# Windowed attention into a gated MLP: a second queue for the block means, another load order, and an order chosen among 64

## The chip, the cores and the metric

The kernel runs on one core of a Trainium2 chip. The metric is the time of the program on the device in microseconds, lower is better. A core has five engines that run side by side, each its own list of instructions in order: TensorE (PE, matrix products), VectorE (DVE), ScalarE (ACT), GpSimd (POOL) and SyncE (SP, which here only issues transfers). Transfers are issued by SP and by ACT; an engine that issues one first waits until the transfer may start, and what stands behind in its list waits too.

## The reference

Four batches of 768 tokens, eight heads of 64. Attention sees two sets of keys: the keys within 16 tokens of the query, and one summary per block of 32 tokens, the maximum of its keys with the mean of its values. An MLP follows, on 3072 tokens of width 512.

```python
k_sum = k.reshape(B, H, nb, block, D).max(axis=3)      # block = 32
v_sum = v.reshape(B, H, nb, block, D).mean(axis=3)
scores_l = where(|i - j| < 16, scale * q @ k.T, -1e9)
scores_s = scale * q @ k_sum.T + log(block)
a = softmax(concat([scores_l, scores_s]))
x = a @ concat([v, v_sum])                             # heads side by side: (3072, 512)
h = x @ w_in                                           # (3072, 1024)
s = h * softmax(h)
ln = (s - mean(s)) / sqrt(var(s) + 1e-6) * g_ln
out = ln @ w_out                                       # (3072, 512)
```

## The kernel before, in words

The work is cut into twelve groups (batch `b`, third `g` of the sequence), each of four query tiles of 64 rows, and each group into two halves `pp` of four heads. A half gives one tile `s` of scores (L555; for the first group straight from `kraw` and `ksum`, else from `kw`, which gathers the windows of keys and the maxima). DVE adds the mask and takes the row minimum (L574), ACT the exponentials (L582), DVE or POOL divides (L265), PE transposes (`t`, L610), ACT or DVE copies to `at`, and PE multiplies with the value tile (`x`, L649). The value tile `vt` of a group holds 96 window rows per query tile, loaded by SP (L512), and below them the 24 block means (`load_v2`, L518), which are copied from `vsum` by a transfer that ACT issues. That transfer writes into the same tile, so it is ordered behind the load.

Each group gives two MLP tile rows of 128 tokens, 24 in all: `h` (L674, two halves of 12 products: four slices of w_in, each in three passes of high and low parts), softmax and centring (L684 to L716; `hm` is the maximum, `he` the tile), transposes `lt` (L610), `lh`/`ll` as high and low part, and `o` (L752, 24 products), which is scaled (L757 or L759) and stored. `o` lags `h` by four tile rows. Both weight matrices come in as words that ACT, DVE and POOL first convert (L345 to L360, L265) and split into a high and a low part (`w`; for w_out L377 and L379). The eight pieces of w_out are thus converted while the first tile rows run, in two buffers that they share with the rows of V that POOL adds for the later batches' means (`st_v`, L478).

Block means are made by PE from rows of V (`vs_ps` with `st_v`, L436) for the first batch, likewise (L449) for the second, and by POOL's sums and PE for the last two.

Nothing runs in the order in which it is written. Every step is recorded with a cost, the engines it could run on, and what it depends on; `Plan.issue` then plays the engines forward. Each engine takes the step that can start first, ties going to the smaller `due` (the earliest place in the program of a PE step that depends on it); `DEAR` is added to an engine's cost where a step could go to several. A transfer is taken to start 1 us after its issue, to move at 410 GB/s (270 at first), and to land 0.6 us later. Where the plan leaves PE idle before 80 us, `keep_up` fills in products with a tile of zeros (L877), so that PE keeps busy; the result is overwritten. `LOADS` sets in which order SP issues the first loads: `k` keys of a pair of heads, `q` queries, `w` a piece of w_in, `r` rows of V for the means, `v` the first value tile, `Q` and `V` the second group's. SP's list is one queue, in order.

Of the kernel before, what the change touches and what calls it, by code (L numbers as in the profile page):

```python
# [2 lines left out]

# [19 lines left out]
NB = S // BLOCK  # L23
# [15 lines left out]
NHE = 5  # L39
EARLY = 3  # L40
MEANS = 2
DIRECT = 0
NEAR = 6
WPT = 2


LOADS = "kqkkqkwwwwwwwwrrrvQV"
NEG = -8.0e9
SCALE = 1.0 / math.sqrt(D)

# [22 lines left out]
class Plan:  # L73
# [4 lines left out]


    RATE, SLOW = 410.0, 270.0  # L80
    START = 0.7
    COLD, FILL = 6.9, 80.0
    IDLE = 0.22
    WAIT, FAR = 1.5, 200
    DEAR = {"dve": 0.6, "act": 0.3, "pool": 1.0}
    SYNC = 0.13

    def __init__(self):
        self.ops, self.rings, self.banks, self.idle = [], {}, {}, None
# [15 lines left out]
    def op(self, engine, cost, fn, r=(), w=(), nbytes=0, after=(), alt=(), port=False):  # L105

        deps = set(after)

        def of(table, part):
            for k, v in table.items():
                if part is None or k is None or k == part:
                    deps.update(v)

        o = Op({e: (c, f) for e, c, f in ((engine, cost, fn), *alt)}, deps,
               len(self.ops), nbytes, port)
        r = [x if isinstance(x, tuple) else (x, None) for x in r]
        w = [x if isinstance(x, tuple) else (x, None) for x in w]
        for b, part in r:  # L120
            of(b.writers, part)
        for b, part in w:
            of(b.writers, part)
            of(b.readers, part)
            for p in b.prev:
                deps.update(p.ops)
                p.gone = True
        assert not any(b.gone for b, _ in r + w)
        for b, part in r:
            b.readers.setdefault(part, []).append(o)  # L130
            b.ops.append(o)
        for b, part in w:
            b.writers.setdefault(part, []).append(o)
            b.ops.append(o)
        deps.discard(o)
        self.ops.append(o)
        return o

    def issue(self):
        ready, free, then, dma, held = {}, {}, {}, 0.0, 0.0  # L140
        for o in self.ops:
            o.left = len(o.deps)
            for d in o.deps:
                d.users.append(o)
        for o in reversed(self.ops):
            o.due = min([u.due for u in o.users] + ([o.prio] if "pe" in o.can else []), default=o.prio)
            if "sp" in o.can:
                o.due = o.prio

        def enter(o):  # L150
            for e in o.can:
                at = max((d.end + (0.0 if d.engine == e == "pe" else self.SYNC) for d in o.deps), default=0.0)
                ready.setdefault(e, []).append((at, o))

        def begin(e, at):
            return max(free.get(e, self.START), at)

        def cost(e, o, t):
            other = free.get("pool", 0.0) if e == "dve" and o.port else held if e == "pool" else 0.0
            return o.can[e][0] * (2 if e == "pe" and t < self.COLD else 1) + max(other - t, 0.0)  # L160

        def loss(e, o, t):
            return cost(e, o, t) + self.DEAR.get(e, 0.0)

        def take(e):

            if e in then:
                return next(((begin(e, at), o) for at, o in ready[e] if o is then[e]), None)
            best = None
            for at, o in ready[e]:  # L170
                t = begin(e, at)
                if any(begin(f, at) + loss(f, o, t) < t + loss(e, o, t) for f in o.can if f != e):
                    continue
                if best is None or t < best[0] - 1e-6 or (t < best[0] + 1e-6 and (o.due, o.prio) < (best[1].due, best[1].prio)):
                    best = (t, o)
            if best is None:
                return None

            t, o = best
            for at, y in ready[e]:  # L180
                s = begin(e, at)
                if t < s and s - t < self.WAIT * (t + cost(e, o, t) - s) and y.due + self.FAR < best[1].due:
                    best = (s, y)
            return best

        for o in self.ops:
            if not o.left:
                enter(o)
        order = []
        while len(order) < len(self.ops):  # L190
            t, e, o = min(((x[0], e, x[1]) for e in ready for x in [take(e)] if x),
                          key=lambda x: (x[0], x[2].due))
            for f in o.can:
                ready[f] = [x for x in ready[f] if x[1] is not o]
            then.pop(e, None)
            if o.then:
                then[e] = o.then
            o.start, o.engine, (o.cost, o.fn) = t, e, o.can[e]
            o.end = free[e] = t + cost(e, o, t)
            if e == "dve" and o.port:  # L200
                held = o.end
            if o.nbytes:
                dma = max(dma, o.end + 1.0)
                dma += o.nbytes / (self.RATE if dma > self.COLD else self.SLOW) * 1e-3
# [6 lines left out]
        at, done = self.START, set()  # L211
        for o in order:
            if o.engine == "pe":
                while at + self.SYNC < min(o.start, self.FILL):
                    at += self.keep_up(at, done)
                at = max(at, o.start) + o.cost * (2 if o.start < self.COLD else 1)
            done.add(o)
            o.fn()

    def keep_up(self, at, done):  # L220

# [10 lines left out]
def attn_then_solu(ctx: ExitStack, tc: tile.TileContext, q, k, v, vr, vb, w_in, w_out, g_ln, out):  # L232
# [281 lines left out]

    def load_v2(b, g):
        x, y = vt[b, g], vsum[b]

        return op(act, 0.8, lambda: nc.scalar.dma_start(  # L518
            out=x.ap[WIN:KC], in_=y.ap[WIN:KC, :].rearrange("p (o c) -> p o c", o=1).broadcast_to([NB, G, DM])),
                  r=[y], w=[(x, 1)], nbytes=NB * 8192)  # L520

    def scores(b, g, pp, direct=False, each=False):

# [290 lines left out]
    step = lambda i: (*its[i // 2], i % 2)  # L814
    for t in range(NT):
        n, j = divmod(t, 2)
        b, g = its[n]
        near = t >= NEAR
        if not near:
            run(scores(*step(t + 2), t < DIRECT))  # L820
# [100 lines left out]
```

## Time and profile before

| | |
|---|---|
| time, median of 3 | 408.04 us (407.03 to 408.69) |
| profiled execution | 406.69 us, span 404.9 us, granted TensorE clock 0.99 |
| PE busy | 388.3 us (96%) |
| of that, products with zeros | 21.6 us in 82 instructions |
| DVE, ACT, POOL busy | 300.5, 230.5, 88.8 us |
| DMA | 49.24 MB, the queue of SP 40.12, that of ACT 8.51 |

The first `h` product starts at 36.31 us, the first `o` product at 74.81. From 136 us on a tile row takes some 14.4 us of PE work, nearly without a wait. A row of the PE timeline names in brackets how long the engine was idle before it and what ended that.

### The profile page before, as it was taken

The numbers are of one execution on the slowest core, as the hardware profiler recorded it, in microseconds if no ns is written. First come the engines' busy times: TensorE is split into PE (matmuls) and PEld (weight loads), VectorE is DVE, ScalarE is ACT, GpSimd is POOL, SyncE is SP. The second block draws the span as 40 slices with busy tenths as digits, with TensorE's granted clock in tenths as the row PEclk, the third lists the DMA queues.
The fourth block names the chain that finished last, engine by engine and source line by source line (L and its number), as shares of the span: only waits on it lengthen the run. The fifth ranks groups of instructions, "written<-read, shape, count | busy, mean of one in ns | idle before, by whom it ended". The sixth has DMA issues, their size and how long they took to land.

```text
span 404.9 us, 9684 instructions
## 1 busy us (share of the span) xinstructions
PE 388.3 (96%) x3702; PEld 299.6 (74%) x3702; DVE 300.5 (74%) x933; ACT 230.5 (57%) x711; POOL 88.8 (22%) x231
## 2 busy tenths in 40 slices
PE   7999999986988999998999999999999999999996
PEld 3436667664876788887888888878878888888776
DVE  4998999989887886776877777687678766654430
ACT  2967788963898664565455664646545453423311
POOL 3020240305581412216202211201201221011100
PEclk9999999996999999999999999999999999999999
DMA  8999992044257040044350040141130000000011
GB/s 270 411 409 364 404 336 75 25 123 152 86 186 258 26 159 28 28 176 126 108 182 21 28 182 2 40 169 42 41 137 2 28 28 26 2 26 28 26 53 52
DMA packets 14994, 49.24 MB, mean 122 GB/s; under 512 B 1836, under 2 KB 2092, under 8 KB 13412
## 3 DMA queue, kind: packets, MB, share of 16 engines
q1 hardware_dynamic: 10112, 40.12, 27.4%
q10 hardware_dynamic: 4836, 8.51, 6.9%
q8 instruction: 29, 0.48, 0.5%
q14 instruction: 17, 0.14, 0.1%
HBM read 40.11 MB, written 6.29 MB: 115 GB/s over the span
## 4 chain that ended last, share of the span: by engine, by line
PE 71%; DMA 12%; DVE 11%; ACT 3%; issue 1%; POOL 1%; SPq 0%; ACTq 0%; POOLq 0%
PE o L752 32%; PE h L674 23%; PE x L649 5%; PE s L555 4%; DMA kraw<-in_k 3%; DMA qt<-in_q 3%; PE lt L610 3%; DMA raw<-in_w_in 2%; PE t L610 2%; DMA vt<-in_v 2%; DMA st_v<-in_vb 1%; DVE e L265 1%; DVE e L574 1%; DVE hm L684 1%; DVE ksum L416 1%
## 5 line engine op out<-in xcount | busy, mean ns | idle before, releaser
L752 PE MATMUL o<-w,lh 128*128 128x512 f32 (+1 forms) x400 | 129.6, 393 | 4.8 <-DVE w L379 4.8
L674 PE MATMUL h<-w,xh 128*128 128x512 f32 x384 | 125.6, 396 | 0.0
L582 ACT ACTIVATE e<-e,nm 128x120 f32<-128x120 f32 x192 | 73.1, 385 | 40.2 <-DVE nm L574 31.1
L752 PEld LDWEIGHTS o<-w,lh 128*128 128x128 f32 x400 | 74.6, 189 | 23.9 <-DVE w L379 5.6
L674 PEld LDWEIGHTS h<-w,xh 128*128 128x128 f32 x384 | 72.1, 188 | 17.4 <-DVE he L697 0.5
L752 PE MATMUL o<-w,ll 128*128 128x512 f32 (+1 forms) x200 | 77.3, 386 | 0.0
L674 PE MATMUL h<-w,xl 128*128 128x512 f32 x192 | 75.5, 393 | 0.0
L684 DVE TENSOR_REDUCE hm<-h 128x1 f32<-128x512 f32 x48 | 32.7, 684 | 33.8 <-PE h L674 33.5
L716 POOL TENSOR_SCALAR ss<-ss 128x1 f32<-128x1 f32 x24 | 6.4, 268 | 167.7 <-ACT sq L712 151.9
L752 PEld LDWEIGHTS o<-w,ll 128*128 128x128 f32 x200 | 38.0, 190 | 6.4
L674 PEld LDWEIGHTS h<-w,xl 128*128 128x128 f32 x192 | 36.1, 188 | 7.8 <-DVE xl L655 0.3
L574 DVE CUSTOM_DVE_ANT_0 e<-s,mask 128x120 f32<-128x120 f32 x192 | 40.6, 276 | 0.1
L689 ACT ACTIVATE he<-h,hm 128x512 f32<-128x512 f32 x48 | 32.8, 691 | 13.9 <-DVE hm L686 13.9
L258 ACT COPY at<-t 120x512 f32<-120x512 f32 x29 | 16.3, 585 | 35.6 <-PE t L610 35.1
L582 ACT ACTIVATION_READ_ACCUMULATOR e<-e,nm 128x1 f32 x192 | 36.4, 190 | 0.0
L697 DVE SCALAR_TENSOR_TENSOR he<-h,hz,he 128x512 f32<-128x512 f32 x48 | 34.2, 744 | 0.2
L737 DVE TENSOR_TENSOR ll<-lt,lh 128x512 fp32r<-128x512 f32 x48 | 31.6, 679 | 0.2
L649 PE MATMUL x<-at,vt 120*64 120x64 f32 (+1 forms) x768 | 28.3, 225 | 0.4 <-DVE at L259 0.4
L265 DVE TENSOR_TENSOR e<-e,z 128x960 f32<-128x960 f32 x24 | 28.5, 1189 | 0.1
L478 POOL TENSOR_TENSOR st_v<-st_v 96x512 f32<-96x512 f32 (+3 forms) x28 | 22.1, 791 | 29.2 <-DMA st_v<-in_vb 28.5
L649 PEld LDWEIGHTS x<-at,vt 120*64 120x64 f32 (+1 forms) x768 | 24.6, 138 | 5.2 <-issue 2.3
L712 ACT ACTIVATE sq<-he 128x1024 bf16<-128x1024 f32 x24 | 25.2, 1050 | 5.3 <-DVE hm L684 2.7
(93 smaller groups left out, 504.2 us busy)
## 6 DMA issues: line engine op xcount, KB each, us to landing
vt<-in_v SPq DMA_DIRECT2D x12, 1024.0 KB, 6.2
kraw<-in_k SPq DMA_DIRECT2D x16, 400.0 KB, 8.5
out<-os ACTq DMA_DIRECT2D x23, 256.0 KB, 2.1
qt<-in_q SPq DMA_DIRECT2D x11, 512.0 KB, 5.4
raw<-in_w_in SPq DMA_DIRECT2D x8, 512.0 KB, 10.1
raw<-in_w_out SPq DMA_DIRECT2D x8, 512.0 KB, 10.1
st_v<-in_vr SPq DMA_DIRECT2D x6, 512.0 KB
st_v<-in_vb SPq DMA_DIRECT2D x8, 384.0 KB, 3.4
```

The source lines that it names most:

```text
L265: by = {dve: lambda: nc.vector.tensor_tensor(out=to(), in0=a(), in1=b(), op=kind), pool: lambda: nc.gpsimd.tensor_tensor(out=to(), in0=a() ...
L478: op(pool, 0.15 + w * 0.0021, lambda w=w, o=o: nc.gpsimd.tensor_tensor(out=o.ap[:n, :w], in0=x.ap[:n, :w], in1=x.ap[:n, w:2 * w], op=ALU.add),
L574: nc.vector.tensor_tensor_reduce(out=e.ap[:, n, :], in0=sc.ap[:, j, (2 * i + up) * KC:(2 * i + up + 1) * KC], in1=mask[:, mi, :], scale=-S ...
L582: nc.scalar.activation(out=e.ap[:, n, :], in_=e.ap[:, n, :], func=AF.Exp, bias=nm.ap[:, n:n + 1], scale=-1.0, accum_out=z.ap[:, n:n + 1])
L649: nc.tensor.matmul(xp()[j * D:(j + 1) * D, i, qs], vs.ap[:k, u, cs], at.ap[:k, u % 2, n[j] + u // 2, :], start=not apart, stop=not apart o ...
L674: nc.tensor.matmul(hp.ap, a.ap[:, c, ts], w.ap[:, i], start=(c == 0 and n == 0), stop=(c == NKC - 1 and n == 2))
L684: op(dve, 0.6, lambda i=i, hp=hp: nc.vector.tensor_reduce(out=nms.ap[:, i:i + 1], in_=hp.ap, op=ALU.max, axis=AX.X, negate=True), r=[hp], ...
L689: op(act, 0.71, lambda i=i, hp=hp: nc.scalar.activation(out=part(i), in_=hp.ap, func=AF.Exp, bias=nm.ap, accum_out=zs.ap[:, i:i + 1]), r=[ ...
L697: op(dve, 0.67, lambda i=i, hp=hp: nc.vector.scalar_tensor_tensor(out=part(i), in0=hp.ap, scalar=zs.ap[:, 0:1], in1=part(i), op0=ALU.mult, ...
L712: op(act, 1.13, lambda: nc.scalar.activation(out=sq.ap, in_=e.ap, func=AF.Square, accum_out=ss.ap), r=[e], w=[sq, ss])
L737: op(dve, 0.6, lambda part=part, r=r: nc.vector.tensor_tensor(out=part(lo), in0=tp.ap[:, r], in1=part(hi).bitcast(F32), op=ALU.subtract), ...
L752: nc.tensor.matmul(o.ap[:, cols], a.ap[:, f, :], w.ap[:, i, cols], start=(f == 0 and n == 0), stop=(f == NFC - 1 and n == 2))
```

## The change

Six things change together.

- `load_v2`: from the second batch on, SP issues the transfer of the block means (at the plan's cost of 0.43 us) and not ACT (0.8 us). The two of the first batch stay with ACT.
- `LOADS`: two pieces of w_in are listed ahead of the first keys, and others are set between the keys and the rows of V.
- `LATE`: the plan lets a transfer that ends after 50 us land 2.0 us after its data and not 0.6.
- `DEAR["dve"]`: 1.0 and not 0.6, so a step that could run elsewhere leaves DVE sooner.
- `issue`: the old loop is now `order`. It runs 64 times, 63 of them with normal noise (3.0, in places of the program) on every `due`, and the order is kept whose last PE step ends first by the plan. An order that gets stuck is dropped.
- `DIRECT` (zero) and its argument go; that changes nothing.

```diff
-LOADS = "kqkkqkwwwwwwwwrrrvQV"
+LOADS = "wwkwqkkkqwwwrrrwwvQV"
+    LATE = 50.0
-    DEAR = {"dve": 0.6, "act": 0.3, "pool": 1.0}
+    DEAR = {"dve": 1.0, "act": 0.3, "pool": 1.0}
+    TRIES, NOISE = 64, 3.0
...
+        due, best = [o.due for o in self.ops], None
+        for seed in range(self.TRIES):
+            noise = random.Random(seed)
+            for o, x in zip(self.ops, due):
+                o.due = x + (noise.gauss(0.0, self.NOISE) if seed else 0.0)
+            order = self.order()
+            if order:
+                end = max(o.end for o in order if "pe" in o.can)
+                if best is None or end < best[0]:
+                    best = end, order, [(o.start, o.end, o.engine, o.cost, o.fn) for o in self.ops]
...
-                o.end = dma + 0.6
+                o.end = dma + (0.6 if dma < self.LATE else 2.0)
...
     def load_v2(b, g):
         x, y = vt[b, g], vsum[b]
-
-        return op(act, 0.8, lambda: nc.scalar.dma_start(
+        e, cost, queue = (sp, 0.43, nc.sync) if b else (act, 0.8, nc.scalar)
+        return op(e, cost, lambda: queue.dma_start(
```

Which engine runs what also changes. Over the program DVE makes 2 `at` copies instead of 19, 18 centrings of `he` instead of 36, and 11 output scalings instead of 18; ACT and POOL have the rest (POOL 11 centrings instead of 1). PE's list has the same products, and 83 products with zeros instead of 82: 72 of them before the first `h` product, where there were 64.

The start of SP's list (`raw` is a piece of a weight matrix as it comes in, `qt` queries, `st_v` rows of V). Before:

```order
L407 DMA kraw_0_93<-in_k 128x800
L506 DMA qt_0_99<-in_q 128x512
L407 DMA kraw_0_93<-in_k 128x800
L407 DMA kraw_1_102<-in_k 128x800
L506 DMA qt_0_99<-in_q 128x512
L407 DMA kraw_1_102<-in_k 128x800
L333 DMA raw_106<-in_w_in 128x1024
```

and with the change:

```order
L356 DMA raw_93<-in_w_in 128x1024
L430 DMA kraw_0_99<-in_k 128x800
L529 DMA qt_0_101<-in_q 128x512 x2
L430 DMA kraw_0_99<-in_k 128x800
L356 DMA raw_105<-in_w_in 128x1024
L356 DMA raw_107<-in_w_in 128x1024
L356 DMA raw_109<-in_w_in 128x1024
L430 DMA kraw_1_111<-in_k 128x800 x2
```

One piece of w_in is first, three more come before the second pair of keys; the rows of V, which were transfers 15 to 17, are 13, 14 and 18.

The end of the conversion of w_out. ACT's list before (`cv_1280` is the last piece, `vt_1_1229` the value tile of the second batch's second group):

```order
L258 CAST lh_1262<-lt_1212 128x8x64
L518 DMA vt_1_1229<-vsum_896 24x4x512
L345 ACTIVATE cv_1280<-raw_272 128x512
L377 ACTIVATE w_1291<-cv_1254,g_sb 128x512
L377 ACTIVATE w_1309<-cv_1280,g_sb 128x512
```

PE's list with the change, where the last piece (`w_1366`) is used for the first time; before, all products of pieces 5 to 8 stood together, with the score group `s_0_1` behind them:

```order
L775 MATMUL o_1118<-w_1258,ll_1072 128x512
L775 MATMUL o_1118<-w_1258,lh_1059 128x512
L633 MATMUL t_0_0_1325<-ident,e_0_0_1132 120x64 x16
L578 MATMUL s_0_1_1344<-kw_0_1_1041,qt_0_536 64x120 x16
L672 MATMUL x_0_0_1376<-at_0_0_1361,vt_0_849 64x64 x16
L775 MATMUL o_1118<-w_1366,lh_1059 128x512
L775 MATMUL o_1118<-w_1366,ll_1072 128x512
```

The transfer of means is gone from this place of ACT's list (on SP it now stands behind one load of rows of V, ahead of the queries of the group after), and transposes, a score group and an `x` stand between the last two pieces.

SP's list around the third value tile, before:

```order
L506 DMA qt_0_624<-in_q 128x1024
L506 DMA qt_2_656<-in_q 128x1024
L512 DMA vt_2_663<-in_v 128x2048
L407 DMA kraw_0_665<-in_k 128x800 x2
L407 DMA kraw_1_696<-in_k 128x800 x2
L407 DMA kraw_0_711<-in_k 128x800 x2
```

and with the change:

```order
L529 DMA qt_0_536<-in_q 128x1024
L430 DMA kraw_0_603<-in_k 128x800 x2
L529 DMA qt_2_698<-in_q 128x1024
L535 DMA vt_2_717<-in_v 128x2048
L430 DMA kraw_0_722<-in_k 128x800 x2
L430 DMA kraw_1_733<-in_k 128x800 x2
```

The first two keys of the third batch (`kraw_0_711`, now `kraw_0_603`) were last of these and are now ahead of the third group's queries and value tile.

More of the change, by code (lines that the diff above doesn't have):

```diff
@@ L1 @@
 import math
+import random
 from contextlib import ExitStack
@@ L41 @@
 MEANS = 2
-DIRECT = 0
 NEAR = 6
 WPT = 2
-LOADS = "kqkkqkwwwwwwwwrrrvQV"
+LOADS = "wwkwqkkkqwwwrrrwwvQV"
 NEG = -8.0e9
@@ L139, in issue @@
     def issue(self):
-        ready, free, then, dma, held = {}, {}, {}, 0.0, 0.0
         for o in self.ops:
-            o.left = len(o.deps)
             for d in o.deps:
@@ L148, in issue, with order @@
                 o.due = o.prio
+        due, best = [o.due for o in self.ops], None
[8 more added lines that the diff above has]
+                    best = end, order, [(o.start, o.end, o.engine, o.cost, o.fn) for o in self.ops]
+        _, order, kept = best
+        for o, x in zip(self.ops, kept):
+            o.start, o.end, o.engine, o.cost, o.fn = x
+        at, done = self.START, set()
+        for o in order:
+            if o.engine == "pe":
+                while at + self.SYNC < min(o.start, self.FILL):
+                    at += self.keep_up(at, done)
+                at = max(at, o.start) + o.cost * (2 if o.start < self.COLD else 1)
+            done.add(o)
+            o.fn()
+    def order(self):
+        ready, free, then, dma, held = {}, {}, {}, 0.0, 0.0
+        for o in self.ops:
+            o.left = len(o.deps)
         def enter(o):
@@ L191, in issue @@
             t, e, o = min(((x[0], e, x[1]) for e in ready for x in [take(e)] if x),
-                          key=lambda x: (x[0], x[2].due))
+                          key=lambda x: (x[0], x[2].due), default=(0.0, None, None))
+            if o is None:
+                return None
             for f in o.can:
@@ L210, in issue @@
                     enter(u)
[L211 to L218, printed above, removed]
+        return order
     def keep_up(self, at, done):
@@ L516, in load_v2 @@
         x, y = vt[b, g], vsum[b]
-        return op(act, 0.8, lambda: nc.scalar.dma_start(
+        e, cost, queue = (sp, 0.43, nc.sync) if b else (act, 0.8, nc.scalar)
+        return op(e, cost, lambda: queue.dma_start(
             out=x.ap[WIN:KC], in_=y.ap[WIN:KC, :].rearrange("p (o c) -> p o c", o=1).broadcast_to([NB, G, DM])),
-                  r=[y], w=[(x, 1)], nbytes=NB * 8192)
+            r=[y], w=[(x, 1)], nbytes=NB * 8192)
     def scores(b, g, pp, direct=False, each=False):
@@ L819, in attn_then_solu @@
         if not near:
-            run(scores(*step(t + 2), t < DIRECT))
+            run(scores(*step(t + 2)))
         if t == NEAR - 1 or (near and j == 0 and n + 3 < len(its)):
```

## The prediction

> **What bounds the kernel now.** I read the page's busy shares and slices first, then the PE waits, then the chain of waits where PE stands still, then windows of the first 100 us.
>
> ```profile
> span 404.9 us, 9684 instructions
> ...
> PE 388.3 (96%) x3702; PEld 299.6 (74%) x3702; DVE 300.5 (74%) x933; ACT 230.5 (57%) x711; POOL 88.8 (22%) x231
> ...
> PE   7999999986988999998999999999999999999996
> ...
> PEclk9999999996999999999999999999999999999999
> ```
>
> PE is the bound: 16.6 us of the span are not PE work. Of these 1.2 lie ahead of its first instruction and 3.0 behind its last product (the final `os` copy starts at 401.87), so some 12.3 us are waits inside: slices 9 to 13 show a notch, and the granted clock drops in slice 10. The waits by name:
>
> ```profile
> PE o L752 <- DVE w L379: 4.8, 2, 2.6
> PE s L555 <- issue: 1.4, 2, 1.3
> ...
> PE s L555 <- POOL st_v L478: 1.0, 1, 1.0
> PE s L555 <- DMA kraw<-in_k: 0.7, 1, 0.7
> PE s L555 <- DVE hz L692: 0.7, 1, 0.7
> PE s L555 <- DVE ksum L416: 0.6, 1, 0.6
> ```
>
> The largest is the wait of the first output product (tile `o`, tile row 0) for the last two converted pieces of w_out. The chain of waits says whose fault it is, and the ACT timeline (last row) and the PE windows (PE busy, granted clock, DMA share, GB/s) say what it costs:
>
> ```profile
> 81.63 6.68 DMA vt<-in_v
> 88.33 0.84 ACTq L518
> 89.21 0.67 ACT cv L345
> 89.91 0.69 DVE cv L356
> ...
> 94.32 0.76 DVE w L379
> 95.12 1.65 PE o L752 x3
> 96.77 1.81 PE s L555 x32
> 98.58 2.33 PE o L752 x6
> ```
> ```profile
> 89.21 0.66 ACT L345 ACTIVATE cv<-raw 128x512 f32<-128x512 f32 x1 [3.11 <-DMA vt<-in_v]
> ```
> ```profile
> 88.00:92.00 4.00, 1.43 (x8) 1.00 0.26 49
> 92.00:95.20 3.20, 1.02 (x4) 0.71 0.46 123
> 95.20:97.00 1.80, 1.80 (x11) 0.50 0.44 107
> 97.00:99.00 2.00, 2.00 (x33) 0.50 0.58 204
> 99.00:100.50 1.50, 1.50 (x5) 0.62 0.51 160
> ```
>
> ACT comes to L518, the transfer of block means into the value tile, and may not issue it before the tile's own load (issued 81.63) has landed at 88.31. It stands 3.11 us, and the conversion of the last w_out piece is queued behind. PE then idles 4.75 us, and the clock falls to 0.50. The slow part is priced by the same work elsewhere (the chain of waits, at a full clock):
>
> ```profile
> 334.81 5.67 PE o L752 x24
> ...
> 401.87 0.47 ACT os L757
> ```
>
> Nine `o` products took 1.65 + 2.33 = 3.98 us instead of 9 x 0.236 = 2.1, one score group 1.81 instead of 1.0 (1.05 in a row below, with its last product's drain): 2.65 us more. So this one place costs 7.4 us.
>
> The other inner waits, placed with the PE timeline: 2.65 us before the first `h` product (0.7 and 0.6 for keys and their maxima, 0.6 for `e`, and the two waits in the rows below), 0.65 in two from 36 to 82 us, 2.7 from 113 to 132 (the 0.7 for `hz`, the 1.3 with no releaser, two smaller), 1.2 later (the 1.0 for POOL at 189.89, and 0.2).
>
> ```profile
> 1.24 4.18 PE L877 MATMUL vs_ps<-zero 128*128 128x512 bf16 x11 [1.24 <-DVE zero L280]
> ...
> 22.23 5.31 PE L436 MATMUL vs_ps<-st_v,sel 128*24 128x512 f32 x12 [0.30 <-DMA st_v<-in_vr]
> ...
> 28.51 1.05 PE L555 MATMUL s<-kw,qt 64*64 64x120 f32 x32 [0.43 <-DMA qt<-in_q]
> ...
> 36.31 0.50 PE L674 MATMUL h<-w,xh 128*128 128x512 f32 x1
> ```
>
> With the clock that is 2.65 + 0.65 + 7.4 + 2.7 + 1.2 = 14.6 us, all that an order can win.
>
> **The change, part by part.** It removes no computation. PE's list holds the same products and 83 fillers (products with `zero`) instead of 82. A filler costs 0.226 us:
>
> ```profile
> 12.34 3.84 PE L877 MATMUL vs_ps<-zero 128*128 128x512 bf16 x17
> ```
>
> So the list is 0.2 us longer, and everything else is waits. I go through the five groups.
>
> *Head, 2.65 now.* The new list has 72 fillers before the first `h` product instead of 64 (+1.8) and one score group more (+1.0). Before, the list took 36.31 - 1.24 - 2.65 = 32.4 us; the new one takes 35.2, so without a wait the first `h` stands at 36.5, with 2.8 us of list more behind it. The loads may not allow that (windows: busy of PE, PEld, DVE, ACT, POOL, clock, DMA share, GB/s):
>
> ```profile
> 0.00:10.00 10.00, 7.36 (x110) 3.82 (x111) 4.21 (x14) 2.37 (x3) 3.97 (x18) 1.00 0.80 267
> 10.00:20.00 10.00, 9.60 (x87) 4.77 (x85) 10.00 (x42) 9.50 (x40) 0.00 (x0) 1.00 1.03 412
> 20.00:30.00 10.00, 9.07 (x71) 3.20 (x69) 9.96 (x19) 6.81 (x13) 2.06 (x6) 1.00 1.02 409
> ```
>
> The transfer of the last rows of V that the means need is the 18th now, with 8.98 MB up to its end. At these rates 6.8 MB are moved by 20 us and 8.98 by 25.4. The first rows of V, 6.87 MB into the old queue, would be there at 20.2 by this sum and PE had them at 22.2: 2 us of lag. So 27.4, and the list is there at 25.0 (11.5 us of list stand between these products and the first `h`): a wait of 2.4. What the early w_in gives (DVE is busy only 4.21 of the first 10 us) is room on DVE and ACT later, not an earlier first `h`. Bounds 0 and 5 (all loads another 2.6 late); I take **2.5 left**, first `h` near 39.
>
> *36 to 82 us, 0.65 now.* Seven fillers fewer there, so less slack if a vector engine is late. Up to the last w_out piece DVE gives away three `at` copies, one `lh`, one `xh`, one subtraction of w (all six like the `at` copy in a row below, 690 ns, some 0.6 back to back), one conversion and one centring of half that: about 4.3 us. It takes on two maxima of `h` of the same width, 1.3. ACT and POOL take these: ACT has room (57%). Bounds 0 and 3; I take **1.0**.
>
> *The w_out stall, 7.4 now.* The L518 of this value tile is SP's now. ACT's conversion starts when its input is there, 3.1 + 0.84 us sooner. Besides, the last three products of this `o` stand behind more of the list: score, transposes and `x` lie between pieces 6 and 7. Even if DVE kept every wait that it has, piece 7 would be ready at 95.1 less 3.0 of DVE work = 92.1; the list reaches it after 84.6 us of PE work at the durations quoted, plus 1.2 at the start, 1.7 for eleven cold fillers (4.18 instead of 2.5), 3.5 of waits and some 2 of small gaps between unlike groups (what the trace shows beyond products and waits from 36 to 82 us): 93. Bounds 0 and 3 (3 is the whole ACT delay back); I take **0.5**.
>
> The Trainium skill, in TensorE: Matmul & The Clock Gate, section on the HAM clock gate, states that the array falls to half rate after an idle window of about 3.4 us and needs about as long of work to return. The trace agrees with 0.50, and comes back by 100.5, some 5 us after work resumed; here two gaps of 2.57 and 2.18 us with a microsecond of products between were enough. By that rule a remaining wait of 0.5 us costs no clock, which is my sum; were the clock's share proportional to the idle time, it would be 0.3 us more.
>
> What the moved issue holds up on SP: behind it stand the queries of the next group and the V rows for POOL. They have slack: SP idles for most of the span, and the queries after this tile's means feed scores 30 us later. It costs nothing while that holds; if SP's wait grew as long as a key load is under way (8.0, below), still nothing.
>
> *113 to 132 us, 2.7 now.* DVE is held by key loads there, and `hm` and `e` are queued behind:
>
> ```profile
> 117.27 7.99 DMA kraw<-in_k
> 125.28 0.95 DVE L416 TENSOR_REDUCE ksum<-kraw 128x24 f32<-128x768 f32 x1 [0.84 <-DMA kraw<-in_k]
> ```
>
> The plan now lets a load after 50 us land 1.4 us later, which covers 0.84, and DVE's list is shorter. Bounds 0 and 4; I take **1.2**.
>
> *Later, 1.2 now.* The same order of POOL and V rows; bounds 0 and 2.5, I take **1.0**. The heavier weight on DVE moves `at` copies and centrings in the steady part (DVE COPY `at` 19 to 2, ACT 29 to 46):
>
> ```profile
> L259 DVE COPY at<-t 120x512 f32<-120x512 f32 x19 | 13.0, 690 | 8.3 <-ACT at L258 8.3
> L258 ACT COPY at<-t 120x512 f32<-120x512 f32 x29 | 16.3, 585 | 35.6 <-PE t L610 35.1 <-DVE at L259 0.5
> L705 POOL TENSOR_SCALAR he<-he,nmu 128x512 f32<-128x512 f32 x1 | 1.7, 1701 | 6.0 <-DVE nmu L700 6.0
> ```
>
> Both halves on ACT make a pair 0.5 us later, and POOL centres ten times more at 1.7 us. `x` reads an `at` made one tile row earlier, 14 us, and `lt` an `he` three rows earlier; that hides both. Uncovered, each `x` would wait 0.5 us, some 18 times: 9 us.
>
> Sum: 2.5 + 1.0 + 0.5 + 1.2 + 1.0 = 6.2 us of waits for 14.6, and 0.2 for the filler: **8.2 us less**. The profiled execution took 406.7 (1.8 outside its span), 1.3 below the median of 408.0. 8.2 off the median is **400**.
>
> **The rivals.** *No waits worth the name:* all five groups near zero, 408.0 - 14.4 = 393.6. For it: the order is the best of 64 by the plan. Against: the plan of before was good as well, and its chip still waited.
>
> *The vector engine sets the pace from 82 to 130 us:* then PE gains only what DVE gains to the last w_out piece, 3.0 of work and some 2 of the 3.1 that ACT stood: 408.0 - 5 = 403. For it: DVE is busy 10.00 of the 10 us from 10 to 20. Against: what it gives away grows with every tile row.
>
> *Won on paper only:* the 64 orders differ by less than the plan errs, waits come up elsewhere, 406 to 410.
>
> *Slower: ACT is held earlier.* The first batch's means still go out from ACT; that of the third value tile now stands on a load behind two key loads of the third batch, and SP may not issue these before DVE and ACT have read the oldest key buffer. Two key loads are 0.8 MB, 2 us: by the sum of the head the tile lands near 53.6 instead of 51.6, about when ACT comes there, at no price. But SP has been held for just such a buffer:
>
> ```profile
> SPq L407 <- ACT kw L258: 12.3, 2, 10.7
> ```
>
> 10.7 us here would hold ACT 10, and PE with it, and the clock another 2.6: 12.6 lost for 8.2 won, 412. It decides from a hold of some 6 us.
>
> **How the numbers follow.** Forecast (396 to 402.5) 0.58; no waits (below 396) 0.10; vector engine (402.5 to 406) 0.16; on paper only 0.08; slower 0.08. Half a per cent, 2 us, is what a measurement can tell: faster 0.84, same 0.08, slower 0.08. The range 394.5 to 406.5 leaves out the far half of the first rival and the last two, and so 2 in 10.
>
> **What would show it.** First `h` near 39 (36.5 to 41); no wait of `o` for w above 1 us and the clock 1.00 from 80 to 105 us; no ACT idle released by a value load near 88; PE idle between its first and last product near 6 us instead of 12. The forecast is wrong if PE's waits there are 10 us or more, or if an ACT wait for the third value tile shows up near 50 us.

## The result and the profile after

The changed kernel takes 397.36 us (median of 4, 397.20 to 397.45); the kernel before, run beside it, 407.53 us (median of 4, 405.41 to 408.69). The ratio is 0.976, 95% interval 0.971 to 0.980: about 10 us or 2.4% faster. The profiled execution took 397.45 us, 9.2 less than that of before.

The page of the changed kernel, with the busy share of PE and the granted clock in 40 slices:

```profile
span 395.7 us, 9677 instructions
...
PE 386.6 (98%) x3697; PEld 298.3 (75%) x3703; DVE 275.4 (70%) x884; ACT 248.7 (63%) x746; POOL 97.9 (25%) x245
...
PE   8999998999999999999999999999999999999996
PEclk9999999999999999999999999999999999999999
```

The notch in slices 9 to 13 and the drop of the clock in slice 10 are gone. The waits of PE by name, in the same kernel (total us, times, longest):

```profile
PE x L672 <- ACT at L281: 1.5, 2, 1.0
PE vs_ps L900 <- DVE zero L303: 1.2, 1, 1.2
PE vs_ps L459 <- DMA st_v<-in_vr: 0.9, 1, 0.9
PE s L578 <- DVE ksum L439: 0.5, 1, 0.5
PE s L578 <- DVE ll L760: 0.4, 1, 0.4
PE h L697 <- DVE he L720: 0.4, 1, 0.4
```

No product `o` waits for w any more. Five windows place the rest. Each row has the stretch, its length, the busy time of PE, PEld, DVE, ACT and POOL with their instructions, the granted clock, the DMA share and GB/s. Before:

```profile
1.24:40.00 38.76, 36.03 (x364) 18.37 (x365) 32.50 (x95) 26.11 (x70) 6.54 (x24) 1.00 1.00 374
40.00:62.00 22.00, 21.74 (x235) 14.67 (x234) 21.52 (x79) 17.31 (x66) 6.79 (x6) 1.00 0.94 359
62.00:80.00 18.00, 17.59 (x197) 12.74 (x196) 18.00 (x64) 16.73 (x45) 2.58 (x9) 1.00 0.17 45
80.00:135.00 55.00, 47.53 (x501) 36.85 (x500) 47.51 (x138) 38.50 (x118) 25.30 (x56) 0.94 0.46 148
135.00:390.00 255.00, 253.61 (x2329) 206.35 (x2329) 178.72 (x559) 129.00 (x412) 47.06 (x133) 1.00 0.20 67
```

The same windows of the changed kernel:

```profile
1.24:40.00 38.76, 36.62 (x390) 18.31 (x396) 33.92 (x113) 29.75 (x94) 12.66 (x29) 1.00 1.00 381
40.00:62.00 22.00, 22.00 (x209) 15.93 (x209) 21.38 (x58) 15.26 (x46) 1.64 (x2) 1.00 0.96 345
62.00:80.00 18.00, 16.13 (x185) 11.41 (x186) 16.27 (x63) 16.62 (x49) 5.60 (x16) 1.00 0.17 47
80.00:135.00 55.00, 54.30 (x611) 42.58 (x610) 48.80 (x150) 48.20 (x145) 29.20 (x60) 1.00 0.50 153
135.00:390.00 255.00, 254.99 (x2300) 207.63 (x2293) 154.72 (x502) 137.47 (x416) 48.20 (x133) 1.00 0.20 68
```

Length less PE busy gives PE's idle time: 2.7, 0.3, 0.4, 7.5 and 1.4 us before, 2.1, 0, 1.9, 0.7 and 0 after, so 12.3 against 4.7. (Six of the changed kernel's 83 products with zeros have no record in this profile, which has 83 of their weight loads and 77 products, five of the six ahead of the first `h`; so up to 1.3 us of the 4.7 may be work.) The clock of 0.94 from 80 to 135 us is 1.00 now. The gain lies from 80 to 135 us: of the 7.5 us of idle time there, 4.75 were the two waits for w_out and 2.7 lay from 113 to 132. From 62 to 80 us PE waits 1.5 us *more* than before. The places, on the PE timeline after:

```profile
20.52 1.88 PE L459 MATMUL vs_ps<-st_v,sel 128*24 128x512 f32 x4 [0.90 <-DMA st_v<-in_vr]
...
26.74 3.61 PE L459 MATMUL vs_ps<-st_v,sel 128*24 128x512 f32 x8
...
38.32 0.50 PE L697 MATMUL h<-w,xh 128*128 128x512 f32 x1
...
66.42 1.15 PE L672 MATMUL x<-at,vt 120*64 120x64 f32 x32 [1.01 <-ACT at L281]
...
93.48 1.04 PE L672 MATMUL x<-at,vt 120*64 120x64 f32 x28 [0.53 <-ACT at L281]
94.45 0.50 PE L775 MATMUL o<-w,lh 128*128 128x512 f32 x1
```

and DVE's timeline, the last converted piece of w_out:

```profile
92.99 0.75 DVE L402 SCALAR_TENSOR_TENSOR w<-cv,g_sb,w 128x512 fp32r<-128x512 f32 x1
```

Before, DVE began that piece at 94.32; it is only 1.3 us earlier now. It ends at 93.74, and PE's list comes to the first product with it at 94.45, after the wait of 0.53 us for an `at` copy in the row above. Without that wait it would be there at 93.92, still 0.2 us behind the piece.

### The profile page after: what moved, and what is told of

The parts are those of the page before. It is cut to its first block, busy times and chain, and to the rows that moved or that the text cites. A ratio compares the mean times of both kernels' runs of the same rounds, so it can differ in the third digit from the quotient of the medians.

```text
span 395.7 us, 9677 instructions
## 1 busy us (share of the span) xinstructions
PE 386.6 (98%) x3697; PEld 298.3 (75%) x3703; DVE 275.4 (70%) x884; ACT 248.7 (63%) x746; POOL 97.9 (25%) x245
## 4 chain that ended last, share of the span: by engine, by line
PE 85%; DMA 6%; ACT 3%; DVE 2%; issue 1%; ACTq 1%; SPq 1%; DVEq 0%
PE o L775 35%; PE h L697 30%; PE x L672 6%; PE s L578 5%; PE t L633 3%; PE lt L633 3%; DMA st_v<-in_vr 3%; DMA raw<-in_w_in 2%; DMA vt<-vsum 2%; PE vs_ps L459 1%; PE x L900 1%; ACT he L712 1%; DVE he L720 1%; ACT at L281 1%; PE x L664 1%
## 5 line engine op out<-in xcount | busy, mean ns | idle before, releaser
L775 PE MATMUL o<-w,lh 128*128 128x512 f32 (+1 forms) x400 | 128.0, 390 | 0.1
L697 PE MATMUL h<-w,xh 128*128 128x512 f32 x384 | 127.0, 398 | 0.4 <-DVE he L720 0.4
L281 ACT COPY at<-t 120x512 f32<-120x512 f32 x46 | 24.8, 587 | 46.1 <-PE t L633 45.6
L288 DVE TENSOR_TENSOR e<-e,z 128x960 f32<-128x960 f32 x23 | 26.6, 1156 | 0.5
L281 ACT CAST lh<-lt 128x512 fp32r<-128x512 f32 x33 | 18.6, 596 | 12.9 <-PE lt L633 10.0
```

Of the source, the lines that this page charges most:

```text
L281: by = {act: lambda: nc.scalar.copy(out=to(), in_=of()), dve: lambda: nc.vector.tensor_copy(out=to(), in_=of()), pool: lambda: nc.gpsimd.t ...
L288: by = {dve: lambda: nc.vector.tensor_tensor(out=to(), in0=a(), in1=b(), op=kind), pool: lambda: nc.gpsimd.tensor_tensor(out=to(), in0=a() ...
L697: nc.tensor.matmul(hp.ap, a.ap[:, c, ts], w.ap[:, i], start=(c == 0 and n == 0), stop=(c == NKC - 1 and n == 2))
L775: nc.tensor.matmul(o.ap[:, cols], a.ap[:, f, :], w.ap[:, i, cols], start=(f == 0 and n == 0), stop=(f == NFC - 1 and n == 2))
```

## The experiments

Two kinds must be kept apart. Some runs change one thing and *hold the order*: every engine issues the same steps in the same order. The others change a rule of the plan, and the plan is made anew, so another order comes with the edit. For these I give the planner's own figure for the end of PE's last product too, by which it chooses. The kernel before has 398.66, the changed kernel 395.02. The kernel before ran beside every set of experiments, with medians of 405.85 to 406.45; the changed kernel ran once, earlier. A difference of a microsecond between it and an experiment is therefore less sure than the spread of the runs makes it look.

### Only the queue of the means

Order of the kernel before held; SP issues the later batches' means.

```diff
 def load_v2(b, g):
-        return op(act, 0.8, lambda: nc.scalar.dma_start(
+        queue = nc.sync if b else nc.scalar
+        return op(act, 0.8, lambda: queue.dma_start(
```

> The kernel before, its order untouched; only the queue that issues the later batches' block means is SP instead of ACT, at the same places. Theory (the hold of ACT is the cause of the largest wait): ACT's 3.11 us near 88 us is gone, PE's wait of o for w falls from 4.8 us to 1.5 or less, the granted clock stays above 0.95 from 80 to 105 us, and the time is 399 to 403 us. Rival (the order is what counts; the late pieces of w_out are late for DVE's sake anyway): the wait stays above 3 us and the time is 405 to 408 us.

Measured: 404.99 us (402.74 to 406.04, 10 runs; the profiled execution is the fastest of them) beside 406.45 for the kernel before (17 runs); ratio 0.996, interval 0.994 to 0.998. The last piece on DVE's timeline, PE's wait for it on PE's, and the window behind:

```profile
92.31 0.75 DVE L379 SCALAR_TENSOR_TENSOR w<-cv,g_sb,w 128x512 fp32r<-128x512 f32 x1
```
```profile
93.11 0.50 PE L753 MATMUL o<-w,lh 128*128 128x512 f32 x1 [2.18 <-DVE w L379]
```
```profile
95.20:97.00 1.80, 1.80 (x19) 1.30 (x12) 1.80 (x8) 0.99 (x2) 1.80 (x3) 0.50 0.59 212
```

ACT's hold is gone and the last piece still comes only 2.0 us sooner: what the hold had cost DVE was one wait of 1.98 us for ACT's `cv` at 89.91, and now DVE works without a gap up to the piece. It is even 0.7 us earlier than in the changed kernel, and yet PE waits, since its list is at that product 2.2 us too soon (0.48 more are waited for the piece ahead). The hold was a part of the stall, not the whole of its cause. Neither forecast holds: the wait is 2.66 us in all, between the theory's 1.5 and the rival's 3, and the time too lies between the two ranges.

### The order without the queue

The reverse: order of the changed kernel held, the means by ACT (`nc.scalar` for `nc.sync` in `load_v2`).

> The changed kernel, its order untouched; only the queue that issues the later batches' block means is ACT again, at the same places in time. Theory (the hold of ACT is the cause): ACT waits for the value tile ahead of the last w_out piece (some 1 to 3 us near 88 us), PE waits behind it, and the time is 399.5 to 403 us. Rival (the new order takes the last piece away from where PE needs it): under 1 us of new PE wait, 397 to 398.5 us.

Measured: 398.08 us (397.59 to 398.69, 4 runs); ratio to before 0.980, interval 0.977 to 0.983. No `o` product waits for w. ACT's timeline shows the moved transfer without the hold of 3.11 us that it cost before:

```profile
88.53 0.84 ACTq L541 DMA_DIRECT2D vt<-vsum  x1
88.72 1.06 ACT L735 ACTIVATE sq<-he 128x1024 bf16<-128x1024 f32 x1
```

The rival's figures hold: the time is in its range, and the one new wait of PE is 0.95 us at 124.33. In this order the queue is worth some 0.7 us. With the two held orders the case is plain: the new order removes the stall at w_out with either queue, and the queue does not remove it in the old order.

### The queue, planned anew

The kernel before with the new `load_v2`, its cost included (plan's end 397.99).

```diff
-        return op(act, 0.8, lambda: nc.scalar.dma_start(
+        e, cost, queue = (sp, 0.43, nc.sync) if b else (act, 0.8, nc.scalar)
+        return op(e, cost, lambda: queue.dma_start(
```

> The kernel before with the issue of the later batches' means moved to SP, and the plan made anew with that (one order, old loads, old costs). Theory: 399 to 403 us, as with the order held, since the ACT hold was the largest loss. Rival (choice among 64 orders and the other costs carry the gain): 404 to 408 us.

Measured: 402.79 us (402.23 to 404.66, 8 runs); ratio 0.992, interval 0.989 to 0.995. The time is in the theory's range, just. The stall is shorter, but there: `o` waits 2.84 us for w at 94.07.

### One order in place of 64

```diff
-    TRIES, NOISE = 64, 3.0
+    TRIES, NOISE = 1, 3.0
```

> The changed kernel with a single order, the one without noise, in place of the best of 64. Theory: within 2 us of the changed kernel, 397.5 to 400 us, since the noise only shuffles what is hidden. Rival (the choice carries the gain): 402 to 408 us. Its list has 88 products with zeros instead of 83, which alone is 1.1 us if PE is never late for them.

Measured: 400.16 us (399.31 to 401.81, 4 runs); ratio 0.986, interval 0.982 to 0.991; plan's end 397.17. PE waits elsewhere: 1.77 us for rows of V at 19.36, 1.20 for queries at 51.57, 1.04 for w at 92.06. The clock stays at 1.00. The time is 0.2 us above the theory's range and 1.8 below the rival's.

### The other four parts, each undone alone

Four edits to the changed kernel, each planned anew:

```diff
-LOADS = "wwkwqkkkqwwwrrrwwvQV"
+LOADS = "kqkkqkwwwwwwwwrrrvQV"
...
-                o.end = dma + (0.6 if dma < self.LATE else 2.0)
+                o.end = dma + 0.6
...
-    DEAR = {"dve": 1.0, "act": 0.3, "pool": 1.0}
+    DEAR = {"dve": 0.6, "act": 0.3, "pool": 1.0}
...
-        e, cost, queue = (sp, 0.43, nc.sync) if b else (act, 0.8, nc.scalar)
+        e, cost, queue = act, 0.8, nc.scalar
```

The old load order:

> The changed kernel with the old load order (queries and keys first, w_in behind them); its order is searched anew with 64 urgencies. Theory A (the vector engine's list up to the last w_out piece decides, and the early w_in gave it room in the first 10 us): the wait of the first output product for w comes back in part, 0.5 to 2 us, and the time is 399 to 401. Rival (the search finds an order of equal worth for either load order): within 1 us of the changed kernel, 396.5 to 398.5, and no output product waits for w over 0.5 us. In both the keys come earlier, so the waits of PE ahead of the first h product fall, and the first h stands near 37.

No later landing:

> The changed kernel without the later landing of loads past 50 us in the plan (0.6 us for all); order searched anew. Theory A (what counts is DVE's list and the w_out pieces): the stall at w_out stays gone; from 113 to 132 us, where before the change DVE stood behind key loads, PE waits 0.5 to 2 us again; 398 to 399.5. Rival (the searched order gives room there without it): 396.8 to 398, no wait of PE over 0.5 us from 110 to 135 us.

The old weight on DVE:

> The changed kernel with the old weight on DVE (0.6 instead of 1.0), so DVE keeps more copies; order searched anew. Theory A (the relief of DVE is what takes the last w_out piece out of PE's way): the first output product waits for w 1.5 to 3 us, the clock falls, 401 to 404. Rival (the search and the means' queue suffice): 397 to 398.5 and no such wait.

All means by ACT, planned so:

> The changed kernel with all transfers of means on ACT again, planned so, with the search over 64 orders. Theory A (order and DVE carry the gain, the queue is worth little beside them): 398 to 399.5, no wait of an output product for w over 1 us. Rival (the queue carries it, since an ACT that stands on a value load is late with w_out's conversion whatever the order): 400.5 to 404 with an ACT idle of 2 us or more on a value load between 80 and 95 us and a wait of o for w behind it.

| undone | time, us | profiled | ratio to before (interval) | longest waits of PE past 40 us |
|---|---|---|---|---|
| load order | 401.49 (400.50 to 403.43) | 403.43 | 0.986 (0.980 to 0.992) | 1.65 for DVE `nm` at 74.41, 1.37 for w at 100.14, 1.23 for `at` at 69.98 |
| later landing | 401.18 (400.34 to 401.50) | 400.34 | 0.986 (0.981 to 0.991) | 1.07 for queries at 51.66, 0.92 for `at` at 109.40, 0.82 for DVE `e` at 121.91 |
| weight on DVE | 402.73 (401.82 to 405.21) | 405.21 | 0.992 (0.989 to 0.995) | 2.30 and 1.54 for `at` at 69.52 and 95.99 |
| queue, planned | 401.10 (400.39 to 402.99) | 400.39 | 0.987 (0.981 to 0.992) | 1.32 for a copied `o` at 95.86, 1.28 at 123.16 (put down to POOL's `y`, a factor of the MLP, which was done 1.0 us before) |

The waits are those of the profiled execution, which is the slowest or the fastest of its set each time.

Most expectations missed. The old load order brings a wait for w in A's range (0.5 to 2), but as one of three late inputs, and the time is 0.5 us above A's. Theory A said that DVE's relief takes the w_out piece out of PE's way. With the old weight on DVE the time is in its range (401 to 404), but no `o` product waits for w at all: the reason is wrong. With the old landing rule A's wait is there and its time is not: DVE is held by a key load again, and PE behind it by 0.82 us, where A had 0.5 to 2. The rows of DVE's and PE's timelines:

```profile
118.91 0.95 DVE L439 TENSOR_REDUCE ksum<-kraw 128x24 f32<-128x768 f32 x1 [0.94 <-DMA kraw<-in_k]
```
```profile
121.91 0.68 PE L633 MATMUL t<-ident,e 64*120 64x64 f32 x16 [0.82 <-DVE e L288]
```

The kernel before has four such waits of DVE from 121 to 131 us (0.47 to 0.84 us each), the changed kernel has none. But the time is 1.7 us above A's range, since other inputs are late at other places. With the means planned for ACT neither mechanism shows.

Each of the four loses 3.7 to 5.4 us, wherever the new order happens to hit a late input. With the 2.8 of the single order the five losses add up to 19.9 us, twice the gain. That alone proves nothing, since parts that need each other can each cost the whole when they are taken away. But what these runs have in common besides is a new draw, and what a draw is worth can be asked by itself.

### Another draw, nothing else

```diff
-            noise = random.Random(seed)
+            noise = random.Random(seed + 200 if seed else 0)
```

> The changed kernel with other noise on the urgencies (63 other draws); its plan ends the last product at 395.03 us by the planner's own reckoning, the changed kernel's at 395.02. Theory B (the rules of the plan carry the gain, any order that the plan holds equal is equal on the chip): 396.9 to 398.5, inner waits of PE near 5 us. Rival (the plan's reckoning errs by several us from order to order, and the changed kernel's order is a good draw, as the four re-planned variants at 401.1 to 402.7 against plans of 394.1 to 396.0 suggest): 399 to 403, inner waits of 6 to 11 us at other places.

Measured: 407.30 us (405.23 to 408.57, 10 runs) beside 405.85 for the kernel before (16 runs); ratio 1.002, interval 1.000 to 1.005. The same rules, the same plan's end to 0.01 us, and the whole gain is gone: worse than the rival asked for. Its page and two windows of its first stage:

```profile
span 406.3 us, 9676 instructions
...
PE 390.9 (96%) x3700; PEld 298.5 (73%) x3700; DVE 273.1 (67%) x875; ACT 249.6 (61%) x747; POOL 107.3 (26%) x253
```
```profile
22.00:24.00 2.00, 1.47 (x2) 0.32 (x3) 2.00 (x13) 2.00 (x11) 0.52 (x1) 0.56 0.98 399
24.00:26.00 2.00, 2.00 (x4) 0.43 (x3) 0.78 (x2) 1.32 (x8) 0.00 (x0) 0.59 1.03 408
```

The five windows used above give 3.6, 0.3, 2.8, 3.3 and 1.1 us of idle PE, 11.1 together against 4.7 in the changed kernel. PE is busy 4.3 us longer, though its list has three products with zeros less (80). Up to 1.3 of the 4.3 are the six records that the changed kernel's profile lacks; the slow clock is another part, by which the twelve products for the means at 22.53 took 6.85 us and not 5.31 as before the change; the rest I have not placed. This is one other draw; the order without noise, under the same rules, took 400.16.

### The search alone

The kernel before with the search and nothing else of the change (plan's end 396.34): the changed kernel with the four edits of the last table together.

> The search over 64 orders alone: load order, weight on DVE, landing rule and the means' queue are those before the change. Its plan ends at 396.34 by the planner's reckoning, against 398.66 before. If the search alone carries the gain: 398 to 399.5 and no wait of an output product for w. If it needs the relief of DVE and the other queue: 402 to 406, with that wait at 2 us or more and a lower clock behind it.

Measured: 402.53 us (401.09 to 403.01, 5 runs); ratio 0.991, interval 0.987 to 0.994. The time is in the second range, without its mechanism: no wait for w is left, the clock is 0.999, and PE waits 2.9 us for DVE's `e` in three places instead.

### What the plan's figure is worth

| kernel | plan's end | time | difference |
|---|---|---|---|
| before | 398.66 | 406.45 | 7.8 |
| before, queue planned | 397.99 | 402.79 | 4.8 |
| before, searched | 396.34 | 402.53 | 6.2 |
| **the change** | 395.02 | 397.36 | 2.3 |
| one order | 397.17 | 400.16 | 3.0 |
| old load order | 396.00 | 401.49 | 5.5 |
| no later landing | 394.05 | 401.18 | 7.1 |
| old weight on DVE | 395.15 | 402.73 | 7.6 |
| means planned on ACT | 395.16 | 401.10 | 5.9 |
| other noise | 395.03 | 407.30 | 12.3 |

In each difference some 4.9 us are the same, since the plan's figure ends with PE's last product: behind it come 3.1 us of the span and 1.8 outside it. The plan's ends differ by 4.6 us in all, and what the chip adds to them by 10. Among the 64 orders of the change the best five lie within 1 us (395.02 to 395.99), so the plan can't tell which of them is fast. The order that it picked is the one with the smallest difference in the table, and that was luck.

### The one buffer of the means

The wait at 66.42 us has a cause that no part of the change touches. The chain of waits of the changed kernel:

```profile
53.50 6.18 DMA vt<-vsum
59.69 1.35 issue
61.04 0.72 ACTq L485
...
63.35 0.68 ACTq L485
64.03 0.05 issue
64.08 0.72 ACT w L400
64.80 0.61 ACT he L732
65.41 0.95 ACT at L281 x2
```

The block means have one buffer. Four transfers by ACT (L485) write the second batch's means into it, and stand until the first batch's last transfer (issued 53.50) has read it. The row of 6.18 us is cut short: it ends at 59.69 because ACT ran out of other work there. The semaphore by which that transfer tells that it is done is complete at 60.98 in the trace, 7.5 us after its issue, and ACT issues at 61.04, after 1.35 us of standing. Then each issue takes 0.7 us of ACT, where the plan counts 0.34, and the `at` copies behind come late. Read in the same way, the transfer took 8.2 us in the order with other noise and ACT stood 0.7; with the old weight on DVE 8.3 and 1.3. (The longer idle times that the profile has for ACT there, 3.67 and 4.22, are mostly the four issues, 2.88 us, which it doesn't count as busy.) Before the change the read took 8.5 us and was over just as ACT came to it. The first expectation below has 6.2, from the chain's row. So two runs with the order held: two buffers, and besides these the four transfers by SP. (`after` keeps the steps that the plan sees behind each other as they were, so that no new order comes up.)

```diff
-        vsum[b] = y = plan.buf(sb, [P, DM], F32, "vsum", 1, f"vsum{b}")
+        vsum[b] = y = plan.buf(sb, [P, DM], F32, "vsum", 2, f"vsum{b}")
...
-               r=[rows], w=[(y, g)], nbytes=6 * 2048)
+               r=[rows], w=[(y, g)], nbytes=6 * 2048, after=vsum[0].ops)
```
```diff
-            op(act, 0.34, lambda g=g: nc.scalar.dma_start(
+            op(act, 0.34, lambda g=g: nc.sync.dma_start(
```

> The changed kernel, its order held on every engine, with two buffers for the block means in place of one. In the changed kernel ACT's four transfers of the second batch's means stand until the first batch's last transfer of means, issued 53.50, has been read out 6.2 us later, and ACT's at copies and the x product at 66.4 come late. Theory C (that wait on the one buffer is what makes x wait 1.0 us, and part of the 0.8 us that follow at 70 and 74): ACT's wait of 1.35 us ahead of 61.04 is gone, x waits 0 to 0.2, time 395.6 to 396.7. Rival (PE meets another late input a little later, the DVE chain to he at 70.45 or the loads): x's wait gone but the time within 0.4 us of the changed kernel, 397.0 to 397.8.

> As the run before it, and the four transfers of the second batch's means are issued by SP instead of ACT, order otherwise held. ACT loses 2.9 us of issuing (four of 0.7) near 61 us besides the wait. Theory C: 395.2 to 396.5, x without a wait, the waits at 70 and 74 us (0.36 and 0.43) smaller than in the changed kernel. Rival: SP issues them one behind the other after a load and the means come later into the fourth value tile, so that x or a transfer waits there: 397 to 398.5.

Measured: 396.22 us (396.02 to 397.05, 5 runs) with two buffers, 395.78 (395.60 to 396.13, 5 runs) with SP as well; the ratios to before are 0.976 (0.973 to 0.979) and 0.974 (0.972 to 0.977). Timelines of ACT and of PE, two buffers:

```profile
59.84 0.73 ACTq L485 DMA_DIRECT2D vsum<-vs  x1
```
```profile
65.73 1.15 PE L672 MATMUL x<-at,vt 120*64 120x64 f32 x32
```

and with SP besides, PE in 40 slices on the page, and the timelines of SP and of PE:

```profile
PE   8999999999999999999999999999999999999996
```
```profile
59.85 3.00 SPq L485 DMA_DIRECT2D vsum<-vs  x4
```
```profile
65.58 1.15 PE L672 MATMUL x<-at,vt 120*64 120x64 f32 x32
```

Theory C holds in both: `x` runs without a wait, and with SP the waits at 70 and 74 us are gone too (PE idle from 62 to 80 us: 1.9 in the changed kernel, 0.45 and 0.04 here). Both are faster than the kernel before beyond doubt. Against the changed kernel they are 1.1 and 1.6 us lower and no run of one overlaps those of the other, but they did not run beside each other, and the ratios' intervals overlap; the profiled spans (395.7, 394.5, 394.0) and the wait that is gone speak for a real gain of 1 us or more.

## Why the prediction was right, and where its reasons were not

The forecast was 400 us, 394.5 to 406.5, faster at 0.84. The time is 397.4, in the range and in the likeliest case. From the profiled execution 8.2 us were expected and 9.2 came (10.2 between the medians). All its signs came true: the first `h`, the clock, no wait of `o` for w, and 4.7 us of idle PE where it had "near 6".

**Head, 2.5 forecast, 2.1 measured, or up to 1.1 less with the missing records.** The first `h` stands at 38.32 ("near 39"). The loads were where the sum had them: the last rows of V were read at 26.74, against 27.4. That the list would wait 2.4 us for them was wrong; it waits 0.9 for the first rows, and none for the last.

**36 to 82 us, 1.0 forecast, 1.9 measured.** The one term too small. The step considered fewer fillers and what the vector engines gain and lose; it had no term for the one buffer of the means, to which ACT came 1.35 us too early in the new order and just in time in the old. The two-buffer runs show that this is where most of it went: 0.45 us of the 1.9 were left, and 0.04 with SP.

**The w_out stall, 0.5 forecast, 0 measured.** The size was right, the share of the causes was not. "The chain of waits says whose fault it is" named the transfer that ACT could not issue. Taking that alone away brought 1.5 us of time and left 2.7 us of the wait with the clock at 0.50. What decided was the step given second: "the last three products of this `o` stand behind more of the list". Its sum had the piece ready at 92.1 and the list there at 93; measured were 93.74 and 94.45, each some 1.5 us later than in the sum, so that the margin of 0.9 it had found (0.7 in the run, 0.5 of it owed to the late `at` copy just ahead) held. That was closer than the forecast thought. The 3.0 us of DVE work given away did not bring the piece forward by as much (1.3 with everything), and the order drawn with the old weight on DVE does without that relief. One reading was wrong without touching the sum: "3.1 + 0.84 us sooner" counts the issue twice, since ACT's idle time of 3.11 (86.10 to 89.21) holds the 0.84 already.

**113 to 132 us, 1.2 forecast, at most 0.2 measured.** From 80 to 135 us 0.7 us are idle, and 0.53 of that is the wait at 93.48. DVE doesn't stand for a key load there any more, as the forecast had it. Whether the landing rule did this is not shown. Without it DVE stands 0.94 us and PE loses 0.82, but in another order; with other noise DVE stands 2.88 us for a key load at 129.93 in spite of the rule, and with only the queue planned anew it doesn't stand there, without the rule.

**Later, 1.0 forecast, 0 measured.** Both halves of `at` on ACT and POOL's centrings (1.0 us each, where the forecast had 1.7) stay hidden: PE is busy 254.99 of 255 us.

**The clock.** It stays at 1.00, as the forecast said.

**The rivals.** No waits at all would have been 393.6; 4.7 us of them are left. "ACT is held earlier" came true in kind, at another wait (a buffer still being read, not a load) and at 1.0 us, not 12.6. "The vector engine sets the pace" didn't come about. "Won on paper only" had 0.08, argued from the size of the plan's error. For this order it is false, but another draw of the same search is just that case, at 407.3. The same rules gave 400.16 with the order without noise and 407.30 with other noise, so no forecast from the rules alone could have been right for all of these. This one worked from the list that the search had produced and its products' places. That the search had drawn a good list was luck, the change's and not the forecast's; whether the same reading of the list with other noise would have found 407 was not tried.

**What stays open.** Why the chip adds 2 us to one plan and 12 to another is shown only in part: ACT standing for the buffer of the means (1.35 us in the changed kernel, none before), its issues (0.7 for 0.34), DVE held by key loads, and the clock after waits.

## What to carry to other kernels

A search over a model picks among orders that the model can't tell apart; time the best few (not tried here), since two siblings of equal plan differ by 10 us on the chip. To learn what a part of such a change is worth, hold the order and change that part alone: undoing a part and planning anew measures the new draw along with it. And the last wait in a chain isn't the cause of a stall until it has been taken away; here the engine behind it had no slack either, and moving the consumer down its list did what the earlier transfer did not.

## What the runs showed of the hardware

Waits of PE shorter than the two of 2.57 and 2.18 us in the kernel before can cost the clock. With the old weight on DVE there is one of 2.30 us at 69.5, then one of 0.27 (PE windows):

```profile
66.00:68.00 2.00, 1.22 (x6) 0.66 (x4) 0.00 (x0) 0.15 (x1) 0.00 (x0) 1.00 0.10 27
68.00:70.00 2.00, 0.46 (x4) 0.27 (x4) 0.50 (x1) 2.00 (x4) 0.76 (x3) 0.90 0.02 6
70.00:72.00 2.00, 1.75 (x32) 1.64 (x34) 2.00 (x5) 1.80 (x6) 1.21 (x4) 0.50 0.47 90
```

The same came after waits of 1.23 and 1.65 us with 3 us of work between (old load order, 0.50 from 76 to 78 us), and after 1.46 and 0.86 (other noise). But a wait of 2.15 us at 19.59, without the landing rule, left it at 1.00, as did the changed kernel's 1.01. Nor do equal waits always do the same: behind 0.71 and 0.61 us in the first 8 us of the kernel before the clock stayed at 1.00, behind 0.67 and 0.61 at the same place of the kernel with the queue planned anew it was 0.50 from 10 to 12 us. In the traces' records of the clock a stretch at 0.50 behind such waits lasts 3.41 us each time, from 69.58 to 73.00 in the run above, and twice that in the kernel before, 93.32 to 100.15. The rule of the Trainium skill that the prediction names, TensorE: Matmul & The Clock Gate, section on the HAM clock gate, has an idle window of about 3.4 us; here the drop comes after single waits shorter than that, so the measurement decides, and what tells 2.30 from 2.15 stays open.

A transfer of 192 KB that reads 24 rows of means, issued by ACT between 51 and 58 us, was done with its source 5.6 to 8.5 us later in seven runs (53.50 to 60.98 in the changed kernel, at a DMA share of 0.95); one issued at 88.33 in the kernel before, at a share of 0.31, after 3.4. Until then the next writer of that buffer stands, with all that is behind it on its engine: 1.35 us of ACT in the changed kernel.
